# Attention scores of 27 row tiles as two-part float16 products, in a fused attention and feed-forward kernel

## The chip, the cores and the metric

The kernel runs on one core of one Trainium2 chip. The metric is the device time of one execution in microseconds (us), lower is better. Engine names are those of the profile: PE is TensorE's matmul stream, PEld its weight loads, DVE is VectorE, ACT is ScalarE, POOL is GpSimd, SP is SyncE, whose queue issues nearly all the DMAs.

## The reference

Batch 8, 8 heads, 576 rows, head size 64, model width 512. Keys and values are averaged over groups of 8 rows, so each head has 72 pooled keys. The attention is joined over the heads, normalized per row, and put through a feed-forward layer of width 2048 with a residual. All inputs are float32 in effect.

```
k_p = k.reshape(B, H, 72, 8, D).mean(axis=3);  v_p likewise
attn = softmax(q @ k_p^T / sqrt(D))
x = (attn @ v_p), heads joined to rows of 512
xn = (x - mean) / sqrt(var + 1e-6) * g
out = x + relu(xn @ w1) @ w2
```

## The kernel before

**Tiling.** The 4608 rows are 36 row tiles of 128; four tiles make a chunk of 512, so there are 9 chunks. A batch has 576 rows, which is four and a half tiles: of the 36 tiles, 32 lie in one batch, and tiles 4, 13, 22 and 31 straddle two. Each product of the feed-forward layer is done in float16 with both operands split into a high and a low part, three matmuls for one; from chunk 2 on the first layer, and from chunk 3 on the second, go through a seven-product scheme on halves (`slot`, line 792, matmuls at line 727; `slot2`, line 933, matmuls at line 950). Chunks 0 and 1 use the plain form (lines 1015 and 1050).

**The scores.** `load_q` (line 439) brings a tile of q, already transposed by the host to 128 rows (two heads of 64) by 4 pairs by 128 columns, in float32. `scores` (line 443) does one float32 matmul per pair of heads against `kblk`, which holds the pooled k of the pair as two blocks of 64 by 72 on a diagonal with zeros beside them: 128 rows by 144 columns. So a tile takes 4 matmuls, and a straddling one 8, of 64 rows of q each, in which the two batches alternate. DVE then takes the row maximum (line 458) and subtracts it (line 461); `probs` (line 468) applies the exponential on ACT (line 470), splits the result into two float16 parts (lines 481 to 497), and hands it to a DMA transpose (line 500). `values` (line 525) multiplies by the pooled v, in float16, with 16 matmuls per tile (lines 537 and 538), normalizes and forms the input of the feed-forward layer, which another DMA transpose turns (lines 614 and 637).

**Pooled k.** For batches 0 and 1 PE pools k (line 1146). For batches 2 to 7 `reduce_k` (line 1077) sums on DVE what `load_k` brought, one pair of heads at a time, and copies the two blocks into `kblk` with two ACT copies (line 1087).

**All-partition maximum.** `all_max` (line 287) rounds a column to powers of two on DVE, spreads it with one small matmul into a bank of the pool `ps_f` (line 294), and reduces it on DVE (line 303). It serves the scales of the weights and of v. The pool `ps_f` has four PSUM banks, which the feed-forward matmuls also use.

**The order.** Nothing is scheduled by the compiler. Each operation is a Python generator that yields between its steps, and the string `START` (lines 56 to 201) lists, token by token, which operation does its next step. The order of the tokens is the order of each engine's queue and of SP's DMA queue. `A.t` steps through the scores and probabilities of tile t, `B.t` through its values, `HK.b.i` and `HV.b.i` prepare half of a batch's k and v, `U` and `E` are the feed-forward products, and `D` streams parts of the second weights in through SP (line 925). `A.t` begins with the load of q for tile t + 2 (line 1070).

```
def stage_a(t):
    if FIRST_Q <= t + 2 < NRUN * TPC:
        load_q(t + 2)
        yield
    yield from scores(t)
    yield
    yield from probs(t)
```

Of the kernel before, what the change touches and what calls it, by code (L numbers as in the profile page):

```python
# [8 lines left out]
F32 = mybir.dt.float32  # L9
# [34 lines left out]
NPE = 2  # L44
HC = CH // 2
# [35 lines left out]
N.1.3 I.1.1 I.1.1 B.8 B.8 HK.3.1 A.10 N.1.2 HV.2.1 HV.2.1 T.1.0.1 I.1.1 T.1.0.1 HK.3.1 HK.3.1 T.1.0.1 HV.2.1
I.1.1 A.11 A.11 A.11 A.10 I.1.3 I.1.3 I.1.1 T.1.0.1 A.11 I.1.1 I.1.3 T.0.1.1 I.1.3 T.1.0.1 T.1.0.1 HV.2.1 I.1.3
HV.2.1 B.8 HV.2.1 B.8 I.1.3 T.0.1.1 I.1.3 A.12 A.12 I.1.1 HK.3.1 HK.3.1 I.1.1 I.1.1 I.1.3 A.11 A.12 B.8 A.11
HV.2.1 I.1.2 I.1.1 HV.2.1 N.1.1 T.1.0.1 HV.2.1 I.1.3 I.1.1 HK.4.0 HV.3.0 HV.3.0 HV.3.0 I.1.1 A.13 HK.4.0 A.13
HV.2.1 T.1.0.1 HV.2.1 A.12 HK.4.0 HK.4.0 O.0.1 A.13 O.0.1 O.0.1 O.0.1 B.8 I.1.0 HV.2.1 HV.2.1 HV.2.1 T.1.0.1
T.1.1 T.1.1 HV.3.0 HV.3.0 B.9 T.1.1 O.0.1 O.0.1 A.11 B.9 B.9 O.0.1 B.9 O.0.1 I.1.0 I.1.2 I.1.2 HV.3.0 HK.4.0
A.12 A.12 I.1.2 I.1.0 HV.3.0 I.1.2 I.1.2 B.9 I.1.0 I.1.0 B.10 HK.4.0 A.13 B.10 B.10 B.9 B.9 B.9 B.9 I.1.2
HV.3.0 B.9 B.9 I.1.0 A.12 I.1.0 I.1.0 A.13 B.10 I.1.2 O.0.1 B.11 I.1.0 B.10 B.10 I.1.0 B.10 I.1.2 B.9 I.1.0
I.1.2 B.9 HV.3.1 HV.3.1 T.1.1 I.1.0 O.1.0 B.11 I.1.2 I.1.2 U.2.1.1 B.11 B.11 A.14 F.0.0.0 A.13 A.13 O.1.0 O.1.0
U.2.0.1 HV.3.1 T.0.1.1 T.0.1.1 HV.3.1 HV.3.1 F.0.0.0 B.11 F.0.0.0 HV.3.1 F.0.0.0 B.11 F.0.0.0 B.11 B.11 B.11  # L90
HV.4.1 U.2.0.1 O.1.0 B.11 O.1.0 U.2.1.1 U.2.1.2 B.11 B.11 U.2.0.2 F.0.0.0 F.0.0.0 F.0.0.0 HV.4.1 HV.4.1 F.0.0.0
F.0.0.0 F.0.0.0 O.1.0 O.1.0 B.11 HV.4.1 F.0.0.0 U.2.1.5 U.2.0.2 U.2.0.2 B.13 O.1.0 HV.4.1 HV.4.1 HV.4.1 U.2.1.2
F.0.1.1 F.0.1.1 U.2.1.6 U.2.1.5 U.2.1.3 T.1.1 U.2.1.6 U.2.1.6 U.2.0.6 U.2.1.2 HV.4.1 F.0.1.1 F.0.1.1 O.1.1
HV.4.0 U.2.1.3 U.2.0.6 U.2.1.3 U.2.1.3 HV.4.0 HV.4.0 HV.4.0 U.2.1.7 F.1.0.1 U.2.1.7 F.1.0.1 F.1.0.1 F.1.0.1
U.2.0.5 U.2.0.6 F.1.0.1 U.2.0.5 U.2.0.7 O.1.1 U.2.1.7 U.2.0.7 U.2.1.7 U.2.0.7 F.1.0.1 HV.4.0 U.2.0.3 O.1.1
U.2.0.7 HV.4.0 U.2.0.3 U.2.0.3 U.2.0.3 HV.4.0 HV.4.0 O.1.1 F.1.0.1 F.1.0.1 F.1.0.1 F.1.0.1 O.1.1 F.1.0.1 O.1.1
U.2.2.1 U.2.0.4 U.2.0.4 F.1.0.1 U.2.2.1 HV.4.1 N.1.0 F.1.1.0 O.1.1 F.1.1.0 U.2.0.4 F.1.1.0 F.1.1.0 F.2.0.0
O.1.1 F.2.0.0 O.1.1 U.2.2.2 O.1.1 F.2.0.0 F.2.0.0 F.2.0.0 F.2.0.0 F.2.0.0 U.2.2.2 U.2.2.2 F.2.0.0 F.2.0.0 O.1.1
F.2.0.0 U.2.2.6 U.2.2.6 U.2.2.6 F.2.0.0 F.2.1.1 B.12 HV.4.1 F.2.0.0 U.2.1.4 B.13 B.13 U.2.3.1 U.2.3.1 F.2.1.1
F.2.1.1 U.2.2.7 F.3.0.1 B.13 U.2.3.2 U.2.3.2 A.14 HV.4.1 HV.4.1 O.1.1 F.2.1.1 U.2.3.2 B.12 A.14 U.2.2.5 P.2.2.0  # L100
U.2.1.4 U.2.1.4 HV.4.1 HK.4.1 U.2.2.5 U.2.2.7 A.14 U.2.2.7 U.2.2.7 P.2.2.0 B.12 U.2.3.5 F.3.0.1 F.3.0.1 A.14
A.14 U.2.3.6 F.3.0.1 U.2.3.5 HV.4.1 HV.5.0 F.3.0.1 U.2.2.4 A.14 B.13 B.12 U.2.3.6 B.12 B.12 U.2.3.3 U.2.3.3
B.12 A.15 U.2.3.6 A.15 B.13 U.2.3.7 U.2.3.7 A.15 A.15 HV.5.0 U.2.2.4 B.13 P.2.0.0 B.13 B.13 B.13 B.13 U.2.3.4
B.13 U.2.3.7 U.2.3.7 B.14 F.3.0.1 P.2.0.0 A.16 N.0.3 F.3.0.1 U.2.3.3 U.2.3.4 U.2.3.4 U.2.3.3 A.15 A.15 B.14
# [12 lines left out]
B.16 HK.6.0 U.3.2.2 B.17 B.17 E.3.0.6 B.17 U.3.2.3 E.3.0.5 A.19 U.3.2.7 B.17 U.3.2.2 B.17 B.17 A.19 HV.5.1
# [86 lines left out]


@with_exitstack
def attn_ffn_kernel(ctx: ExitStack, tc: tile.TileContext, qT, kn, vn, kT, v, g, w1, w2, out):
    nc = tc.nc

    const = ctx.enter_context(tc.tile_pool(name="const", bufs=1))  # L210
# [1053 lines left out]
```

## Time and profile before

| what | value |
|---|---|
| median of 3 runs | 817.8 us (817.46 to 817.96) |
| span of the profiled execution | 817.1 us |
| PE busy | 794.2 us, 97% of the span |
| DVE busy | 632.6 us, 77% |
| ACT busy | 459.4 us, 56% |
| POOL busy | 297.8 us, 36% |
| mean granted TensorE clock | 0.983 of full |

The span runs from the first to the last instruction of the one profiled execution. The three runs are timed without a profile and differ from that span by what lies around it, 0.7 us at the median. An engine's busy time is the union of its instructions; a matmul's length in the trace reaches to its modelled end, so the pace of matmuls is read from the distance between two starts, not from their length.

### The profile page before, as it was taken

How to read it: one execution, taken by the hardware profiler on the slowest of the kernel's cores; microseconds unless marked ns; L12 is line 12 of the kernel's file. 1: busy time of each engine (PE TensorE's matmuls, PEld its weight loads, DVE VectorE, ACT ScalarE, POOL GpSimd, SP SyncE). 2: the span in 40 equal slices, each digit the busy share in tenths (PEclk: the TensorE clock that was granted, in tenths of full speed). 3: DMA queues.
4: the chain of work that ended last, by engine and by line, in shares of the span. 5: the costliest groups of instructions: out<-in, count | busy, mean ns of one | idle time of the engine just before them, and what ended most of it. 6: DMA issues, size and time to landing. Idle time of an engine off the chain costs nothing.

```text
span 817.1 us, 16797 instructions
## 1 busy us (share of the span) xinstructions
PE 794.2 (97%) x6554; PEld 624.6 (76%) x6554; DVE 632.6 (77%) x1363; ACT 459.4 (56%) x890; POOL 297.8 (36%) x270
## 2 busy tenths in 40 slices
PE   6978999999999999999999999999999999999998
PEld 5857755544566666679889989988988899888887
DVE  1799899677866877599968898889777968976564
ACT  2699966444523362575745755756555756563442
POOL 1222456871354362234332432333322433350211
PEclk9778999999999999999999999999999999999999
DMA  9956988734642247766775586564844473543323
GB/s 324 381 194 215 265 264 264 196 106 101 121 107 101 105 112 166 177 178 166 169 171 152 145 185 156 149 166 111 172 129 93 121 165 92 120 95 97 91 65 104
DMA packets 205214, 128.49 MB, mean 157 GB/s; under 512 B 123104, under 2 KB 182480, under 8 KB 202064
## 3 DMA queue, kind: packets, MB, share of 16 engines
q1 hardware_dynamic: 204992, 127.30, 58.1%
q8 instruction: 51, 0.84, 0.4%
q14 instruction: 27, 0.22, 0.1%
q10 hardware_dynamic: 144, 0.13, 0.0%
HBM read 76.55 MB, written 19.92 MB: 118 GB/s over the span
## 4 chain that ended last, share of the span: by engine, by line
PE 89%; DVE 6%; DMA 2%; ACT 2%; issue 1%; SPq 0%; DVEq 0%; ACTq 0%
PE ps_f L727 28%; PE ps_f L950 26%; PE ps_f L1050 15%; PE ps_f L1015 9%; PE ps L448 4%; PE ps_f L1152 2%; PE ps_f L1168 1%; PE ps L537 1%; PE ps L538 1%; PE ps L535 1%; DMA w<-in_kn_dram 1%; DMA w<-d2B 1%; DMA vr<-in_v_dram 1%; DVE ring L785 1%; DVE w L310 0%
## 5 line engine op out<-in xcount | busy, mean ns | idle before, releaser
L950 PE MATMUL ps_f<-w,ring 128*128 128x256 f16 x2016 | 228.8, 273 | 1.4 <-DVE ring L772 1.2
L950 PEld LDWEIGHTS <-ring 128*128 128x128 f16 x2016 | 196.2, 98 | 25.6 <-DVE ring L772 1.9
L727 PE MATMUL ps_f<-zz,w 128*128 128x256 f16 x1344 | 159.7, 273 | 1.9 <-ACT ps_f L802 1.3
L727 PEld LDWEIGHTS <-w 128*128 128x128 f16 x1344 | 130.7, 98 | 19.4 <-issue 2.5
L1050 PE MATMUL ps_f<-w,ring 128*128 128x512 f16 x576 | 127.4, 379 | 0.0
L727 PE MATMUL ps_f<-zz,raw 128*128 128x256 f16 x1008 | 120.7, 273 | 0.0
L779 POOL TENSOR_TENSOR ring<-v,ring 128x512 f16<-128x512 f32 x48 | 56.4, 1179 | 147.9 <-ACT ring L776 113.5
L727 PEld LDWEIGHTS <-raw 128*128 128x128 f16 x1008 | 98.2, 98 | 12.8 <-issue 0.2
L1050 PEld LDWEIGHTS <-ring 128*128 128x128 f16 x576 | 56.0, 98 | 64.1
L1015 PE MATMUL ps_f<-zz,w 128*128 128x512 f16 (+1 forms) x480 | 87.3, 340 | 1.2 <-DVE allmax L303 1.2
L1015 PEld LDWEIGHTS <-w 128*128 128x128 f16 x480 | 47.1, 99 | 36.6 <-issue 1.4
L489 POOL TENSOR_TENSOR phl<-e,phl 128x512 f16<-128x512 f32 x31 | 36.1, 1163 | 87.2 <-ACT phl L481 83.8
L635 POOL TENSOR_TENSOR hl<-z,hl 128x512 f16<-128x512 f32 x28 | 33.6, 1215 | 72.1 <-ACT hl L633 70.1
L563 ACT ACTIVATE x<-ps,rs 128x64 f32<-128x64 f32 x144 | 33.3, 316 | 32.5 <-DVE x L555 24.4
L448 PE MATMUL ps<-kblk,q 128*128 128x144 f32 (+1 forms) x320 | 45.1, 306 | 4.6 <-issue 3.7
L448 PEld LDWEIGHTS ps<-kblk,q 128*128 128x128 f32 (+1 forms) x320 | 40.0, 191 | 8.3 <-issue 6.3
L577 ACT ACTIVATE z<-x,nb,y 128x512 f32<-128x512 f32 x36 | 29.3, 815 | 30.3 <-DVE nb L572 30.1
L779 POOL TENSOR_TENSOR ring<-ring 128x512 f16<-128x512 f32 x24 | 28.2, 1176 | 49.1 <-ACT ring L776 45.1
L1090 DVE TENSOR_REDUCE vp<-vr 72x64 f32<-72x512 f32 x48 | 32.4, 675 | 10.2 <-DMA vr<-in_v_dram 10.0
L776 ACT CAST ring<-v 128x512 f16<-128x512 f32 x48 | 29.6, 618 | 7.6 <-DVE v L785 3.7
L481 ACT CAST phl<-e 128x1024 f16<-128x1024 f32 x31 | 32.4, 1046 | 2.3 <-DMA pt<-phl 1.4
L517 DVE TENSOR_SCALAR a<-y,ve 128x1 f32<-128x1 f32 x108 | 29.5, 273 | 3.9
(174 smaller groups left out, 1307.1 us busy)
## 6 DMA issues: line engine op xcount, KB each, us to landing
w<-d2T SPq DMA_DIRECT2D x28, 512.0 KB
raw<-in_w_dram SPq DMA_DIRECT2D x12, 1024.0 KB
w<-d2B SPq DMA_DIRECT2D x24, 512.0 KB
q<-in_qT_dram SPq DMA_DIRECT2D x36, 256.0 KB
out_dram<-x SPq DMA_DIRECT2D x32, 256.0 KB
kr<-in_kT_dram SPq DMA_DIRECT2D x24, 288.0 KB
vr<-in_v_dram SPq DMA_DIRECT2D x48, 144.0 KB
ring<-in_w_dram SPq DMA_DIRECT2D x4, 1024.0 KB
```

What stands on the lines that cost most here:

```text
L448: nc.tensor.matmul(ps[r, p // 2, p % 2 * 2 * KV : (p % 2 + 1) * 2 * KV], lhsT=q[:, p, r], rhs=kblk[b % NKB][:, p, :], start=True, stop=True,)
L481: nc.scalar.copy(out=ph[:, :, :, 0:KA], in_=e[:, :, 0:KA].unsqueeze(1).broadcast_to([P, 2, H, KA]))
L489: nc.gpsimd.tensor_tensor(out=ph[:, 0, :, KA:P], in0=e[:, :, 0:KA], in1=ph[:, 0, :, 0:KA], op=ALU.subtract)
L563: nc.scalar.activation(out=xh[:, 4 + i, :], in_=px[:, 1, i, 0:D], func=AF.Copy, scale=rs[:, 4 + i : 5 + i])
L635: nc.gpsimd.tensor_tensor(out=hl[:, 1, r], in0=part, in1=hl[:, 0, r], op=ALU.subtract)
L727: nc.tensor.matmul(ps[:, j], lhsT=w_form(wb, int(m == 2), k)[:, fs], rhs=z_form(za, int(m == 1), k), start=(first and i == 0 and j == 0), ...
L776: nc.scalar.copy(out=hi, in_=src)
L779: eng.tensor_tensor(out=lo, in0=src, in1=hi, op=ALU.subtract)
L950: nc.tensor.matmul(parts[i], lhsT=h[:, hp, f, i * P : (i + 1) * P], rhs=w[:, f // FPB, wp, f % FPB], start=(first and f == k == 0 and (i = ...
L1015: nc.tensor.matmul(ps, lhsT=w[:, part, fs], rhs=zT[:, kz, cols], start=(n == 0), stop=(n == 3 * NKT - 1),)
L1050: nc.tensor.matmul(ps, lhsT=h[:, part, i, cols], rhs=w[:, wp, j], start=(n == 0), stop=(n == 3 * NFT // 2 - 1),)
L1090: nc.vector.tensor_reduce(out=vp[b][:, h, 0:D], in_=vraw.pop((b, h)), axis=AX.X, op=ALU.add,)
```

## The change

Tiles 0 to 8 (batches 0 and 1) keep the float32 scores. From tile 9 (`HQ`) on, q comes in by rows (`qn`, 128 rows by 512) and is split on the chip: the new operation `QS.t` (`split_q`) sums the absolute values of each row on ACT, makes a power-of-two scale per row on DVE, writes the scaled high part in float16 on ACT and the low part on DVE, side by side for each head (64 columns high, 64 low), and turns the 128 by 1024 result with a DMA transpose on SP's queue. `KS.b` (`split_k`) does the like with the pooled k of a batch, with one scale per batch through `all_max`: high and low parts go to the rows of the head's own half, and two DMAs copy them to the other half. A head's scores are then two accumulating float16 matmuls with the same 128 by 128 weights (the high part of q over its low part) and 72 columns each: first the high part of k, then its low part. There are no zero blocks. The scales come out in the exponential, whose factor is now a column made by one more DVE instruction per segment. `reduce_k` writes into a tile that holds all four pairs and no longer needs its ACT copies.

`START` is a new order throughout, from the first line on. It has the tokens of before, less the steps that fell away (27 of the `A` steps, the loads of q, and 36 of `HK`), plus 6 tokens for each of `QS.9` to `QS.35` and `KS.2` to `KS.7`. The flags that choose an engine (the last number of some tokens) are the same for every operation. `QS.t` takes three buffers of the pool tile `q` (rows of q, split q, turned q), and the pool has three.

```
+HQ = 9
...
+    def split_q(t):
+        q = q_tile()
+        nc.sync.dma_start(out=q, in_=qn[t])
+        yield
+        e, s = wk3.tile([P, 1], F32, name="qe"), scalar_tile("s1")
+        hl = q_tile()
+        nc.scalar.activation(out=hl, in_=q, func=AF.Abs, accum_out=e)
+        qe[t] = e
+        yield
+        pow2_floor(e, e)
+        pow2_inverse(s, e, 13)
+        yield
+        hl = hl.bitcast(F16).rearrange("p (h a d) -> p h a d", a=2, d=D)
+        q = q.rearrange("p (h d) -> p h d", d=D)
+        nc.scalar.activation(out=hl[:, :, 0], in_=q, func=AF.Copy, scale=s)
+        yield
+        nc.vector.scalar_tensor_tensor(
+            out=hl[:, :, 1], in0=q, scalar=s, in1=hl[:, :, 0], op0=ALU.mult, op1=ALU.subtract
+        )
+        yield
+        q_sb[t] = qt = q_tile().bitcast(F16).rearrange("p (h n) -> p h n", n=P)
+        nc.sync.dma_start_transpose(out=qt, in_=hl.rearrange("p h a d -> p (h a d)"))
...
+    def scores_f16(t):
+        q = q_sb.pop(t)
+        ps = ps_2.tile([P, 2, 512], F32, name="ps_2")
+        for r, b in segments(t):
+            k = k_parts(b)
+            for h in range(H):
+                o = ps[r, h // 4, h % 4 * KV : (h % 4 + 1) * KV]
+                for a in range(2):
+                    nc.tensor.matmul(o, lhsT=q[:, h, r], rhs=k[:, a, h], start=(a == 0), stop=(a == 1))
+        return ps
...
     def scores(t):
+        ps = scores_f32(t) if t < HQ else scores_f16(t)
         yield
...
         nc.vector.tensor_reduce(out=mx, in_=sc, axis=AX.X, op=ALU.max)
+        if t >= HQ:
+            for r, b in segments(t):
+                nc.vector.tensor_scalar(
+                    out=qe[t][r], in0=qe[t][r], scalar1=EXP_SCALE * 2.0**-26, scalar2=CK[b][r],
+                    op0=ALU.mult, op1=ALU.mult,
+                )
...
-        nc.scalar.activation(out=e, in_=e, func=AF.Exp, scale=EXP_SCALE)
+        nc.scalar.activation(out=e, in_=e, func=AF.Exp, scale=EXP_SCALE if t < HQ else qe.pop(t))
...
     def stage_a(t):
-        if FIRST_Q <= t + 2 < NRUN * TPC:
+        if FIRST_Q <= t + 2 < HQ:
...
-        kp = wk1.tile([P, DM // 2], F32, name="zs")[:, :KV]
...
-            nc.scalar.copy(out=kblk[b % NKB][r, p, c], in_=kp[r])
+        nc.vector.tensor_reduce(out=kp_all[:, p], in_=kr, axis=AX.X, op=ALU.add)
+
+    def split_k(b):
+        m, s = scalar_tile("mv"), scalar_tile("sv")
+        nc.vector.tensor_reduce(out=m, in_=kp_all, axis=AX.XY, op=ALU.max, apply_absolute_value=True)
+        e = yield from all_max(m)
+        pow2_inverse(s, e, 13)
+        CK[b] = wk3.tile([P, 1], F32, name="ck")
+        nc.vector.tensor_copy(out=CK[b], in_=e)
+        yield
+        k = k_parts(b).rearrange("q a (p j) k -> q j a p k", j=2)
+        rows = [slice(j * D, (j + 1) * D) for j in range(2)]
+        for j, r in enumerate(rows):
+            nc.scalar.activation(out=k[r, j, 0], in_=kp_all[r], func=AF.Copy, scale=s[r])
+        yield
+        for j, r in enumerate(rows):
+            nc.vector.scalar_tensor_tensor(
+                out=k[r, j, 1], in0=kp_all[r], scalar=s[r], in1=k[r, j, 0], op0=ALU.mult, op1=ALU.subtract
+            )
+        yield
+        for j, r in enumerate(rows):
+            nc.sync.dma_start(out=k[rows[1 - j], j], in_=k[r, j])
...
-        "qT": q.transpose(1, 3, 0, 2).reshape(NPAIR, P, NTT, P).transpose(2, 1, 0, 3),
+        "qT": q.transpose(1, 3, 0, 2).reshape(NPAIR, P, NTT, P).transpose(2, 1, 0, 3)[:HQ],
+        "qn": q.transpose(0, 2, 1, 3).reshape(NTT, P, DM),
```

## Rows read from the trace of the kernel before

**Rows 1.** The page, part 1: busy time, share of the span, instructions.

```profile
PE 794.2 (97%) x6554; PEld 624.6 (76%) x6554; DVE 632.6 (77%) x1363; ACT 459.4 (56%) x890; POOL 297.8 (36%) x270
```

**Rows 2.** Stretch, its length, then busy PE, PEld, DVE, ACT, POOL; clock, DMA share, GB/s.

```profile
0.00:120.00 120.00, 103.87 (x657) 79.50 (x658) 92.29 (x195) 87.94 (x150) 40.19 (x39) 0.89 0.82 271
120.00:300.00 180.00, 179.98 (x1130) 102.48 (x1129) 138.02 (x296) 82.97 (x162) 92.57 (x69) 1.00 0.51 139
300.00:700.00 400.00, 398.38 (x3727) 342.82 (x3726) 327.51 (x731) 237.65 (x482) 135.48 (x136) 1.00 0.61 149
```

**Rows 3.** The page, part 4: the chain that ended last, by engine.

```profile
PE 89%; DVE 6%; DMA 2%; ACT 2%; issue 1%; SPq 0%; DVEq 0%; ACTq 0%
```

**Rows 4.** PE in order of time, 560 to 600 us: scores and what follows them.

```profile
564.77 1.15 PE L448 MATMUL ps<-kblk,q 128*128 128x144 f32 x8
565.75 1.47 PE L727 MATMUL ps_f<-zz,w 128*128 128x256 f16 x12
567.06 5.72 PE L950 MATMUL ps_f<-w,ring 128*128 128x256 f16 x48
...
597.31 1.20 PE L448 MATMUL ps<-kblk,q 128*64 128x144 f32 x16
598.44 1.48 PE L727 MATMUL ps_f<-zz,w 128*128 128x256 f16 x12
```

**Rows 5.** PE in order of time, 444 to 445 us: `all_max`, then one tile's values.

```profile
444.34 0.20 PE L294 MATMUL ps_f<-ident,rowmax 72*128 72x72 bf16 x1
444.38 0.19 PE L537 MATMUL ps<-va,pt 128*128 128x65 f16 x1
...
444.86 0.19 PE L538 MATMUL ps<-vb,pt 88*128 88x65 f16 x1
444.89 0.27 PE L950 MATMUL ps_f<-w,ring 128*128 128x256 f16 x1
```

**Rows 6.** PE in order of time, 466 to 468 us: values of straddling tile.

```profile
466.14 0.22 PE L537 MATMUL ps<-va,pt 128*64 128x65 f16 x1
...
467.19 0.50 PE L727 MATMUL ps_f<-zz,w 128*128 128x256 f16 x3
```

**Rows 7.** Groups by line and shape, DVE: busy us, mean ns, idle before.

```profile
L520 DVE TENSOR_SCALAR y<-a,y 128x1 f32<-128x1 f32 x108 | 23.1, 214 | 3.8
L772 DVE SCALAR_TENSOR_TENSOR ring<-v,ring 128x512 f16<-128x512 f32 x24 | 16.9, 704 | 0.7 <-ACT ring L770 0.7
L310 DVE SCALAR_TENSOR_TENSOR vb<-vp,sv,vh 72x512 f16<-72x512 f32 x7 | 5.9, 842 | 1.2 <-ACT vh L308 1.2
L272 DVE TENSOR_SCALAR rowmax<-rowmax 72x1 int32<-72x1 int32 x7 | 1.0, 150 | 0.2
```

**Rows 8.** Groups by line and shape, ACT: busy us, mean ns, idle before.

```profile
L633 ACT CAST hl<-z 128x512 f16<-128x512 f32 x28 | 17.1, 619 | 10.7 <-DVE z L626 5.4 <-DMA out_dram<-x 3.7 <-DVE z L628 1.6
L1087 ACT COPY kblk<-zs 64x72 f32<-64x72 f32 x48 | 11.9, 247 | 10.5 <-DVE zs L1081 10.3
L357 ACT ACTIVATION_READ_ACCUMULATOR raw<-w 128x1 f32 x12 | 2.3, 190 | 0.0
```

**Rows 9.** Busy time in two stretches of 20 us, columns as in rows 2.

```profile
440.00:460.00 20.00, 20.00 (x196) 18.16 (x194) 18.41 (x44) 12.60 (x26) 6.23 (x6) 1.00 0.67 180
540.00:560.00 20.00, 20.00 (x196) 18.06 (x195) 18.13 (x44) 10.03 (x18) 6.41 (x6) 1.00 0.62 155
```

**Rows 10.** Transposes of line 614 on SP: duration ns min/median/max, first and last start.

```profile
L614 SPq DMA_TRANSPOSE zz<-hl x14: 1232/1256/1815, 182.9 to 720.3; - x14
```

**Rows 11.** SP's queue, its longest wait: what ended it, us, times, longest.

```profile
SPq L925 <- PE ps_f L950: 93.2, 23, 9.7
```

**Rows 12.** The page, part 3: the DMA queue, packets, MB, share of 16 engines.

```profile
q1 hardware_dynamic: 204992, 127.30, 58.1%
```

**Rows 13.** PE's longest waits: what it waited for, us, times, longest.

```profile
PE ps_f L1152 <- DMA w<-in_kn_dram: 6.9, 1, 6.9
...
PE ps_f L950 <- DVE ring L772: 1.2, 2, 0.9
```

More of the change, by code (lines that the diff above doesn't have):

```diff
@@ L206, in attn_ffn_kernel @@
 @with_exitstack
-def attn_ffn_kernel(ctx: ExitStack, tc: tile.TileContext, qT, kn, vn, kT, v, g, w1, w2, out):
+def attn_ffn_kernel(ctx: ExitStack, tc: tile.TileContext, qT, qn, kn, vn, kT, v, g, w1, w2, out):
     nc = tc.nc
@@ L241, in attn_ffn_kernel @@
     ]
-    pool_w = const.tile([P, 2 * D + P // POOL], F32, name="pool_w")
+    kp_all = const.tile([P, NPAIR * KV], F32, name="kp_all")
+    pool_w = kp_all[:, : 2 * D + P // POOL]
+    kp_all = kp_all.rearrange("p (a k) -> p a k", k=KV)
     ones = pool_w[:, D : D + P // POOL]
@@ L424, in split_v @@
             nc.sync.dma_start(out=VB[b][KV + i * KR : KV + (i + 1) * KR], in_=vh[KA:])
[L427 removed]
+    q_sb, E, PT, X, Z, zTs, qe, CK = {}, {}, {}, {}, {}, {}, {}, {}
     def segments(t):
@@ L441, in load_q, with q_tile, k_parts, scores_f32 @@
         nc.sync.dma_start(out=q_sb[t], in_=qT[t])
-    def scores(t):
+    def q_tile():
+        return wk3.tile([P, NPAIR, P], F32, name="q").rearrange("p a n -> p (a n)")
+    def split_q(t):
[20 more added lines that the diff above has]
+        nc.sync.dma_start_transpose(out=qt, in_=hl.rearrange("p h a d -> p (h a d)"))
+    def k_parts(b):
+        k = kblk[b % NKB].rearrange("p a k -> p (a k)").bitcast(F16)
+        return k.rearrange("p (a h k) -> p a h k", a=2, k=KV)
+    def scores_f16(t):
[8 more added lines that the diff above has]
+        return ps
+    def scores_f32(t):
         q = q_sb.pop(t)
@@ L454, in scores @@
                 )
+        return ps
+    def scores(t):
+        ps = scores_f32(t) if t < HQ else scores_f16(t)
         yield
@@ L1079, in reduce_k @@
         kr = kraw.pop((b, p))
-        kp = wk1.tile([P, DM // 2], F32, name="zs")[:, :KV]
-        nc.vector.tensor_reduce(
-            out=kp, in_=kr, axis=AX.X, op=ALU.add
-        )
-        yield
-        for j in range(2):
-            r, c = slice(j * D, (j + 1) * D), slice(j * KV, (j + 1) * KV)
-            nc.scalar.copy(out=kblk[b % NKB][r, p, c], in_=kp[r])
+        nc.vector.tensor_reduce(out=kp_all[:, p], in_=kr, axis=AX.X, op=ALU.add)
[6 more added lines that the diff above has]
+        nc.vector.tensor_copy(out=CK[b], in_=e)
+        yield
+        k = k_parts(b).rearrange("q a (p j) k -> q j a p k", j=2)
[10 more added lines that the diff above has]
+            nc.sync.dma_start(out=k[rows[1 - j], j], in_=k[r, j])
     def reduce_v(b, h):
@@ L1100, in prep_k @@
             yield
-            yield from reduce_k(b, p)
+            reduce_k(b, p)
             yield
@@ L1216, in attn_ffn_kernel @@
         "LK": rows_k, "LV": rows_v, "G": load_g, "K": pe_k, "V": pe_v, "R": load_raw,
-        "Q": load_q, "A": stage_a, "B": values, "C": convert, "M1": max_w1, "M2": max_w2, "S": split_w, "E": slot2, "D": w2_stream, "J": w2_resident,
+        "Q": load_q, "QS": split_q, "KS": split_k, "A": stage_a, "B": values, "C": convert, "M1": max_w1, "M2": max_w2, "S": split_w, "E": slot2, "D": w2_stream, "J": w2_resident,
         "F": w2_forms, "N": keep_w2, "OUT": put_out,
```

287 lines of the change are left out of this document (142 added, 145 removed).

## The prediction, made before the changed kernel ran

> **What bounds the kernel now.** I read the page's busy times first: PE is busy 97% of the span, no other engine above 77% [rows 1]. A busy PE can still be a slow one, so I then read the stages. From 120 to 700 us PE has no gaps to speak of: 398.4 of 400 us in the long middle, at the full granted clock [rows 2]. Only the first 120 us are loose, with 16 us of idle PE and a mean clock of 0.89, while DVE and ACT are at 77% and 73% and DMA at 82%: four resources near their limits together. The chain of waits says the same, 89% PE [rows 3], and PE's waits are the first load, 6.9 us, and little else: behind DVE's evictions of the middle it loses 1.2 us in all [rows 13]. So in the middle a microsecond taken from PE is a microsecond gained, as long as DVE, busy 327.5 of those 400 us [rows 2], keeps up.
>
> The profiled execution spans 817.1 us; the median of the runs is 817.8, so I add 0.7 at the end.
>
> **PE.** In the middle a whole tile's float32 scores start at 564.77 and the next work at 565.75: 0.98 us for 4 matmuls, each in two records. A straddling tile takes 598.44 less 597.31, 1.13 us [rows 4]. The new form has 16 matmuls per whole tile, float16, 128 by 128 weights, 72 columns. The nearest thing in the trace is one tile's values: 16 float16 matmuls of 65 columns, each with its own weight load, from 444.38 to 444.89, that is 0.51 us or 32 ns each [rows 5]. For 7 more columns at the 2.4 GHz of this stretch I add 3 ns: 35 ns, 0.57 us per tile. Bounds: 0.51 us (columns don't count) and 16 x 109 ns = 1.75 us (every one at the pace of the 256-column matmuls behind that tile, 12 of them from 565.75 to 567.06 [rows 4]). I take 0.57, because the row with the same type, weights and nearly the same width is much the nearest. Gain 0.41 us for each whole tile. A straddling tile becomes 32 matmuls on 64 columns of weights; 32 such in the values take 467.19 less 466.14, 1.05 us [rows 6], so about 1.15 with the wider rows: nothing gained, since the old ones alternated between two batches and were cheap already.
>
> Of tiles 9 to 35, three straddle (13, 22, 31) and 24 don't: 24 x 0.41 = 9.8 us off PE. The six new `all_max` matmuls take 444.38 less 444.34, 0.04 us each [rows 5], 0.2 us in all. Net 9.6 us.
>
> The Trainium skill, TensorE: Matmul & The Clock Gate, section "Back-to-back issue gap", speaks against that: a stream of weight load and matmul pairs is said to sustain about 81 ns per matmul at 128 columns, far above the time of the columns. By it a tile would take some 1.3 us (an estimate from that page), and nothing would be gained. This case's values run at 32 ns with a weight load for each, so the trace doesn't agree.
>
> **DVE.** Added per tile: three small instructions for the power of two (0.15 each by the masking one), the low part of 128 by 512 (0.70), the factor of the exponential (0.21) [rows 7]: 1.36 us, and 0.21 more on straddling tiles. 27 x 1.36 + 0.6 = 37 us. Per batch `KS` adds eight DVE instructions, at least 0.15 and at most 0.84 each [rows 7]; four are single columns, and the other four are bounded by both ends, so 1.2 to 4.0 us; I take 2.3, six batches 14 us. `reduce_k` sums as before. In all 51 us, DVE goes from 633 to 684 us. About 20 of the 27 tiles and four batches fall in the middle, 35 us: 362 us of DVE against 400 less 8 us of PE, 92.5%. In the two densest stretches of before DVE ran 18.41 and 18.13 of 20 us (92% and 91%) with PE at 20.00 [rows 9]. So the load fits, with no slack. I charge 2 us for PE waiting on late evictions; bounds 0 and the DVE rival below.
>
> **ACT.** Added per tile: sum of absolute values and scaled copy (0.62 each by the float16 cast of that size) and the accumulator's read (0.19): 27 x 1.43 = 39 us. Removed: 48 copies, 11.9 us [rows 8]; 12 scaled copies of k come back, bounded by 0.25 and 0.62, say 5. ACT ends near 491 us of 810, 61%. I cost this at nothing because DVE and PE are both denser; without that cover it would be 32 us.
>
> **DMA and SP.** The loads of q are as many and as large as before; they are `QS` tokens now. New are 27 transposes of 1024 columns, 1.26 us each on SP by line 614's [rows 10], 34 us of issue, and 12 small copies of k. SP's queue has slack: its second-weight loads alone stand 93 us waiting for PE to free their place [rows 11]. 1024 packets of 256 B per transpose make 27,648, 13% more than the queue's 204,992 at 58.1% [rows 12], so DMA goes to at most 66%. I cost both at nothing.
>
> **New waits.** `QS` waits for its q on ACT, for ACT on DVE, for DVE on SP, and PE's scores wait for the turned q and, once per batch, for the copies of k. Behind the waiting scores on PE stands the whole feed-forward stream; behind the waiting transpose on SP stand the w2 loads, v loads and outputs. The three q buffers hold about one tile in the making. The chain of five steps takes some 10 us if each queue serves it within 2 us, and a tile comes every 18 us or so (400 us for 22 tiles), so there is room. In the new order the first `QS` token of a tile stands at a median of 36 us of PE work ahead of its scores (token list, priced by rows 4 to 6), and 0 to 28 us lie after its transpose. The few at zero are where I would look for gaps; the old order puts some `B` tokens as close behind their transposes, and no wait on them shows among PE's longest [rows 13].
>
> **The new order early on.** The tokens before the first feed-forward work are the same in sum (41 to 45 us of PE work, 42 to 43 of DVE, 47 of ACT). I take no change; with 16 us of idle PE there and half clock in parts, it may be 5 us either way.
>
> **Sum.** 817.1 - 9.6 + 2 + 0.7 = 810.2, say 810.
>
> **The rivals.**
>
> *DVE becomes the bound (slower).* Place: 300 to 700 us. It decides if DVE can't be kept above 362/400 = 90.5% busy over the whole stretch, since below that the stretch grows past its 400 us. At 88% the stretch is 412 us and the time 817.8 + 12 - 2 (the tiles before it) = 828; at the 82% of now it would be 442 us and 858. For it: dependent hops between ACT and DVE, which no order removes. Against: 92% with PE full in [rows 9]. Chance 0.11.
>
> *The gain is handed back (no change).* Turned q comes late or SP's queue blocks the w2 loads: a wait of 0.35 us in each of the 27 tiles is 9.5 us. Time 813 to 819, centre 817. For it: a chain of five queues with three buffers. Against: the distances above. Chance 0.14.
>
> *The change doesn't shorten the matmuls.* If each small matmul goes at the pace of its weight load rather than of its columns, by the upper bound a whole tile costs 0.77 us more and a straddling one 32 x 0.109 - 1.13 = 2.4 more: 817.8 + 18.5 + 7 = 843; halfway, 824. Against: rows 5. Chance 0.03. The skill's 81 ns would give about 830.
>
> *The new order also closes early gaps.* A third of the 16 idle us goes: 803 to 805. Chance 0.10.
>
> **How the numbers follow.** Forecast 0.62, at 810 (806 to 813 by itself). Some 0.2% (1.6 us) is what a measurement can tell from no change: faster means below 816.2, slower above 819.4. Faster: 0.62 + 0.10 + 0.08 of the handed-back case = 0.80. No change: the other 0.06. Slower: 0.11 + 0.03 = 0.14. The range goes from 804 to 818.5: it leaves out the slower cases and the best of the early-gap case, about 0.2.
>
> **What would show it right or wrong.** Right: 16 score matmuls of 128x72 f16 some 35 ns apart, a tile's scores 0.57 us; PE busy down by 9 to 10 us; DVE 680 to 690 us and ACT about 490; PE still above 99% in the middle. Wrong: small matmuls 60 ns apart or more; PE waiting several us in all for DVE's evictions (lines 748, 772, 779, 785) or for a transposed q; a first 120 us with more or less PE work done than now.

## The result, and the profile after

Time after: 807.8 us median (804.3 to 809.2, four runs), against 817.9 (817.5 to 818.0) beside it. The ratio is 0.9867 with a 95% interval of 0.9844 to 0.9890, so the change saves 9 to 13 us. A second set on another chip gave 806.0 against 818.7, ratio 0.9835 (0.9817 to 0.9853). Forecast were 810, with 804 to 818.5 as the range. The profiled execution took 807.3 us; its span of 805.6 stands against 817.1. Of the experiments below, three hold one execution that is a quarter to several times longer than its neighbours (the old form of the scores, the maximum replaced, the scaled copy three times), which their medians and ratios leave out.

The page's busy times, its DMA queue and the engines' shares of the chain that ended last, after the change:

```profile
PE 781.4 (97%) x6800; PEld 610.4 (76%) x6800; DVE 675.2 (84%) x1549; ACT 489.1 (61%) x935; POOL 306.1 (38%) x270
...
q1 hardware_dynamic: 239840, 135.26, 64.9%
...
PE 78%; DVE 11%; DMA 5%; ACT 4%; issue 1%; POOL 0%; SPq 0%; DVEq 0%; ACTq 0%
```

Against [rows 1, 3, 12]: PE is busy 12.8 us less, its idle time went from 22.9 to 24.2 us (span less busy), and the difference is the 11.5 us of the span. The chain tells what the time alone doesn't: PE's share fell from 89% to 78%, and DVE, DMA and ACT hold 20% of it, where they had 10. The kernel still ends on PE, but other engines are on its path far more often.

The same by stage, columns as in [rows 2]:

```profile
0.00:120.00 120.00, 106.11 (x659) 77.43 (x660) 91.44 (x201) 88.10 (x149) 31.67 (x35) 0.90 0.79 274
120.00:300.00 180.00, 175.60 (x1249) 100.50 (x1247) 157.54 (x362) 92.43 (x179) 102.31 (x73) 1.00 0.65 162
300.00:700.00 400.00, 397.81 (x3956) 341.67 (x3955) 362.32 (x864) 263.65 (x527) 146.36 (x140) 1.00 0.70 162
```

In the long middle DVE went from 327.5 to 362.3 us (90.6%) and PE still has only 2.2 us of gaps. New gaps stand between 120 and 300 us, 4.4 us where there were none; the first 120 us have 2.2 fewer than before.

What the change was made for, PE in order of time: a whole tile's scores and what follows them, two times, then a straddling tile's (compare [rows 4]).

```profile
530.23 0.68 PE L482 MATMUL ps<-kblk,q 128*128 128x72 f16 x16
530.74 1.48 PE L779 MATMUL ps_f<-zz,w 128*128 128x256 f16 x12
...
550.91 0.68 PE L482 MATMUL ps<-kblk,q 128*128 128x72 f16 x16
551.43 1.48 PE L779 MATMUL ps_f<-zz,w 128*128 128x256 f16 x12
...
395.01 1.12 PE L482 MATMUL ps<-kblk,q 128*64 128x72 f16 x32
396.07 0.21 PE L295 MATMUL ps_f<-ident,rowmax 72*128 72x72 bf16 x1
```

From start to start a whole tile takes 0.51 to 0.52 us, 32 ns for each of its 16 matmuls, where the float32 form took 0.98. A straddling tile takes 1.06 instead of 1.13.

The largest groups of the new steps by line and shape: busy us, mean ns, idle before. First PE's scores (float16 at line 482, what is left of float32 at line 490), then the low part of q on DVE and its scaled copy on ACT.

```profile
L482 PE MATMUL ps<-kblk,q 128*128 128x72 f16 x384 | 16.4, 198 | 0.0
L482 PE MATMUL ps<-kblk,q 128*64 128x72 f16 x96 | 3.4, 200 | 0.0
L490 PE MATMUL ps<-kblk,q 128*128 128x144 f32 x64 | 11.2, 328 | 0.8 <-ACT x L615 0.8
L490 PE MATMUL ps<-kblk,q 128*64 128x144 f32 x16 | 2.2, 454 | 0.0
...
L463 DVE SCALAR_TENSOR_TENSOR q<-q,s 128x512 f16<-128x512 f32 x27 | 22.3, 827 | 1.8 <-ACT q L461 1.7
...
L461 ACT ACTIVATE q<-q,s 128x512 f16<-128x512 f32 x27 | 19.5, 722 | 9.6 <-DVE s L279 9.5
```

PE's scores before, as groups:

```profile
L448 PE MATMUL ps<-kblk,q 128*128 128x144 f32 x256 | 39.3, 299 | 0.9 <-ACT kblk L1162 0.9
L448 PE MATMUL ps<-kblk,q 128*64 128x144 f32 x64 | 5.8, 332 | 3.7 <-issue 3.7
```

The scores sum to 33.2 us of PE instead of 45.1 (39.3 + 5.8). PE waited for nothing in front of the new ones: their idle time is 0.0.

PE's longest waits after (what it waited for, us, times, longest; before in [rows 13]):

```profile
PE ps_f L1218 <- DMA w<-in_kn_dram: 6.7, 1, 6.7
PE ps_f L640 <- ACT z L629: 4.3, 2, 2.8
PE ps_f L1102 <- DVE w L311: 2.3, 2, 1.5
PE ps_f L295 <- DVE ring L1081: 1.6, 1, 1.6
```

None of them is for a turned q or a copy of k. The first is the load at the start, as before. The second, PE's transposes of the first tiles waiting for ACT at about 57 and 61 us, has no like before. The fourth is the new `all_max` of a batch's k at 181.8 us (128 by 128, like the five other new ones; those of v are 72 by 72), held until DVE was through with an eviction of line 1081. So one of the new steps does make PE wait, for 1.6 us. The third is new too. Three more views show its cause: the split of the second weights in the profile of before (ns, min/median/max), then DVE in order of time, then POOL, around 140 us after the change.

```profile
L310 DVE SCALAR_TENSOR_TENSOR w<-w,ws x8: 1271/1276/1305, 107.2 to 145.1; 128x1024 f16<-128x1024 f32 x8
```

```profile
139.37 3.27 DVE L311 SCALAR_TENSOR_TENSOR w<-w,ws 128x1024 f16<-128x1024 f32 x1
142.55 0.67 DVE L1156 TENSOR_REDUCE vp<-vr 72x64 f32<-72x512 f32 x1
143.85 1.85 DVE L311 SCALAR_TENSOR_TENSOR w<-w,ws 128x1024 f16<-128x1024 f32 x1 [0.62 <-ACT w L309]
```

```profile
138.29 1.16 POOL L650 TENSOR_TENSOR hl<-z,hl 128x512 f16<-128x512 f32 x1 [7.00 <-ACT hl L648]
139.41 2.14 POOL L726 TENSOR_TENSOR w<-w 128x1024 f32<-128x1024 f16 x1
141.63 2.99 POOL L729 TENSOR_TENSOR w<-w 128x1024 f32<-128x1024 f32 x1
```

The split of the second weights on DVE, 1.27 to 1.31 us each in the profile of before, took 3.27 and 1.85 here. POOL's sum of line 726 ends at 139.41 + 2.14 = 141.55, and 1.09 us behind that the first of them is done; line 729 ends at 144.62, and the second is done 1.08 behind that. So the new order put a DVE instruction with two inputs in SBUF beside POOL instructions that read SBUF, and by these ends DVE stood until POOL was through. The Trainium skill, SBUF — State Buffer, section "Who interferes with whom", says that a DVE instruction with two SBUF inputs contends with a GpSimd instruction that reads SBUF, and calls it an exclusive lock; the 3.27 us agree with it.

### The profile page after: what moved, and what is told of

Its sections match the earlier page's. It is cut to its first block, busy times and chain, and to the rows that moved or that the text cites. A ratio compares the mean times of both kernels' runs of the same rounds, so it can differ in the third digit from the quotient of the medians.

```text
span 805.6 us, 17573 instructions
## 1 busy us (share of the span) xinstructions
PE 781.4 (97%) x6800; PEld 610.4 (76%) x6800; DVE 675.2 (84%) x1549; ACT 489.1 (61%) x935; POOL 306.1 (38%) x270
## 3 DMA queue, kind: packets, MB, share of 16 engines
q1 hardware_dynamic: 239840, 135.26, 64.9%
## 4 chain that ended last, share of the span: by engine, by line
PE 78%; DVE 11%; DMA 5%; ACT 4%; issue 1%; POOL 0%; SPq 0%; DVEq 0%; ACTq 0%
PE ps_f L779 30%; PE ps_f L1002 24%; PE ps_f L1102 10%; PE ps_f L1067 6%; DMA vr<-in_v_dram 2%; DVE w L311 2%; PE ps L482 1%; PE ps_f L1218 1%; PE ps L589 1%; PE ps_f L1234 1%; PE ps L590 1%; PE ps L587 1%; DMA kr<-in_kT_dram 1%; DMA w<-in_kn_dram 1%; DVE vp L1156 1%
## 5 line engine op out<-in xcount | busy, mean ns | idle before, releaser
L1067 PE MATMUL ps_f<-zz,w 128*128 128x512 f16 (+1 forms) x480 | 85.2, 336 | 0.7 <-DVE w L311 0.7
L504 DVE TENSOR_REDUCE mx<-ps 128x8 f32<-128x576 f32 x36 | 27.0, 750 | 11.9 <-PE ps L490 8.5
L343 POOL TENSOR_SCALAR raw<-raw 128x1024 int32<-128x1024 uint16 x12 | 14.5, 1208 | 48.9 <-DMA raw<-in_w_dram 39.7
```

Source lines behind the costliest of these rows:

```text
L1067: nc.tensor.matmul(ps, lhsT=w[:, part, fs], rhs=zT[:, kz, cols], start=(n == 0), stop=(n == 3 * NKT - 1),)
```

## The experiments

Three theories. **PE**: the gain is the shorter scores, in a kernel that PE bounds. **DVE**: DVE is now a bound too, and hands part of it back or is near doing so. **Order**: the order found anew brings time of its own. Times of different chips are compared through the kernel before beside them, 818 to 819 us each time.

**The old form of the scores in the new kernel.** All of the new preparation runs in the new order, but the scores use the float32 matmuls of before on the bits that lie there, so that scores, and output, are others. (The exponent of both scales, of q and of k, is made smaller, to keep the numbers finite.)

```diff
-        pow2_inverse(s, e, 13)
+        pow2_inverse(s, e, 3)
...
-        for r, b in segments(t):
-            k = k_parts(b)
-            for h in range(H):
...
+        q = q.rearrange("p h n -> p (h n)").bitcast(F32).rearrange("p (a n) -> p a n", n=P)
+        for p in range(NPAIR):
+            for r, b in segments(t):
+                nc.tensor.matmul(
+                    ps[r, p // 2, p % 2 * 2 * KV : (p % 2 + 1) * 2 * KV],
+                    lhsT=q[:, p, r],
+                    rhs=kblk[b % NKB][:, p, :],
...
```

> The changed kernel, with one thing undone: from tile 9 on the scores are again 4 float32 matmuls of 144 columns per whole tile (8 on a straddling one), reading the bits of the split q and k as float32, so they are no scores; the power-of-two scales are 2^10 smaller to keep them finite. All splits, transposes, DVE and ACT work and the whole new order stay. Theory PE (the gain is PE's shorter scores): 24 whole tiles x (0.98 - 0.51) + 3 x 0.1 = 11.5 us more than the changed kernel, about 819. Rival ORDER (a good part of the gain is the new order): at most half of that, 813 or less.

Measured: 817.7 us median of nine, ratio 0.9988 (0.9974 to 1.0002). Its scores in PE's order of time, and its long middle:

```profile
535.14 1.15 PE L480 MATMUL ps<-kblk,q 128*128 128x144 f32 x8
536.13 1.47 PE L783 MATMUL ps_f<-zz,w 128*128 128x256 f16 x12
...
300.00:700.00 400.00, 398.96 (x3717) 342.57 (x3716) 355.83 (x853) 258.80 (x515) 142.78 (x138) 1.00 0.70 159
```

With scores of 0.99 us the whole gain is gone. So the net gain is PE's. This run also prices all that was added: 45 us of DVE (677.6 against 632.6 busy), 30 of ACT, 27 transposes and a new order together come to no change (0.9974 to 1.0002). It gives their sum only: what the new order brings by itself may be offset by what the new steps cost. In its profile PE is idle for 27.8 us instead of the 22.9 of before, and the mean clock of the first 120 us is 0.96 instead of 0.89. So Order falls as the source of the net gain, not as a term within it.

**Every score matmul twice.** The second pair starts its sum anew, so the result is the same.

```diff
-                for a in range(2):
+                for a in (0, 1, 0, 1):
```

> The changed kernel with every float16 score matmul done twice over (start, accumulate, start, accumulate), same result. Theory PE: 24 x 0.51 + 3 x 1.05 = 15.4 us more, about 823. Rival DVE (DVE at 90% of the middle sets the time, PE fills in): PE would have slack for it, under 8 us more.

Measured: 824.1 us, ratio 1.0071 (1.0049 to 1.0092), some 17 us above the changed kernel.

```profile
539.39 1.20 PE L482 MATMUL ps<-kblk,q 128*128 128x72 f16 x32
540.43 1.48 PE L779 MATMUL ps_f<-zz,w 128*128 128x256 f16 x12
...
300.00:700.00 400.00, 399.38 (x4199) 343.48 (x4198) 355.12 (x844) 257.82 (x513) 139.25 (x135) 1.00 0.70 158
```

32 matmuls take 1.04 us, 0.52 more than 16. Over 24 whole and 3 straddling tiles that is 24 x 0.52 + 3 x 1.06 = 15.7 us, and nearly all that the time rose by (on the page PE's busy time rose by 14.8, from 781.4 to 796.2). PE's time counts about in full, in both directions. With PE longer, DVE has slack again: 355 of 400 us, and PE's gaps in the middle shrink to 0.6.

**The low part of q twice on DVE.**

```diff
-        nc.vector.scalar_tensor_tensor(
-            out=hl[:, :, 1], in0=q, scalar=s, in1=hl[:, :, 0], op0=ALU.mult, op1=ALU.subtract
-        )
+        for _ in range(2):
+            nc.vector.scalar_tensor_tensor(
+                out=hl[:, :, 1], in0=q, scalar=s, in1=hl[:, :, 0], op0=ALU.mult, op1=ALU.subtract
+            )
```

> The changed kernel with the low part of q written twice on DVE: 27 x 0.65 = 17.5 us of DVE more, 13 of it in the middle, which brings DVE from 362 to about 375 of 400 us there. Theory PE: DVE still fits, 0 to 3 us more, at most 811. Rival DVE: the added work comes out in full, about 17 us more, 825.

Measured: 825.7 us, ratio 1.0082 (1.0050 to 1.0114): 17.9 above 807.8. The doubled group and two stretches of it:

```profile
L464 DVE SCALAR_TENSOR_TENSOR q<-q,s 128x512 f16<-128x512 f32 x54 | 48.6, 900 | 2.7 <-ACT q L461 1.7
...
120.00:300.00 180.00, 170.89 (x1184) 95.03 (x1183) 159.34 (x360) 93.05 (x180) 102.17 (x72) 1.00 0.66 165
300.00:700.00 400.00, 389.16 (x3834) 328.89 (x3832) 371.97 (x858) 254.84 (x508) 143.63 (x135) 1.00 0.70 159
```

DVE gets to 372 of 400 us, 93.0%; PE now stands 10.8 us in the middle and 9.1 before it, in many waits of 0.2 to 2.5 us: 10.5 of these 20 us for DVE, 3.4 for ACT, 5.7 for DMAs, of which 0.9 for turned q, which the second write makes later. The group rose by 26.3 us (48.6 against 22.3) and DVE's busy time by 26.1, more than the 17.5 expected, since the 54 writes took 900 ns on average. So 26 us more of DVE cost 18. The theory that PE alone binds, whatever DVE does, falls.

**The low part of q left out.** ACT writes the high part into both halves.

```diff
-        nc.scalar.activation(out=hl[:, :, 0], in_=q, func=AF.Copy, scale=s)
+        nc.scalar.activation(out=hl, in_=q.unsqueeze(2).broadcast_to([P, H, 2, D]), func=AF.Copy, scale=s)
...
-        nc.vector.scalar_tensor_tensor(
-            out=hl[:, :, 1], in0=q, scalar=s, in1=hl[:, :, 0], op0=ALU.mult, op1=ALU.subtract
-        )
```

The changed kernel ran once more beside it, as it stands:

> The changed kernel once more, as the yardstick for the three beside it. Both theories: 808 us, about 10 under the kernel before.

> The low part of q is left out of the computation (both halves hold the high part): 17.5 us less DVE, about 12 us more ACT, PE's work the same. If the changed kernel is bound by PE alone, with DVE only just keeping up, it gains no more than the gaps that DVE causes: 0 to 4 us (804 to 808). If DVE is a second bound of the middle, on which every us counts as in the run with the low part twice, it gains 8 to 10 us (798 to 800).

Measured: 806.0 us and 801.3; ratios 0.9835 (0.9817 to 0.9853) and 0.9781 (0.9758 to 0.9805). DVE's busy time fell by 18.4 us, so 18 us less of DVE are worth about 5, against 18 for 26 us more. Where the 5 lie: the page's busy times and the first two stretches, first of the changed kernel, then without the low part.

```profile
PE 781.7 (97%) x6800; PEld 610.3 (76%) x6800; DVE 675.6 (84%) x1549; ACT 488.3 (61%) x935; POOL 305.3 (38%) x270
...
0.00:120.00 120.00, 105.31 (x655) 76.98 (x656) 90.66 (x200) 87.48 (x147) 30.90 (x35) 0.90 0.80 271
120.00:300.00 180.00, 175.92 (x1250) 100.73 (x1249) 157.14 (x361) 92.67 (x181) 103.11 (x73) 1.00 0.67 164
```

```profile
PE 775.5 (97%) x6800; PEld 606.0 (76%) x6800; DVE 657.2 (82%) x1522; ACT 499.3 (62%) x935; POOL 300.3 (38%) x270
...
0.00:120.00 120.00, 102.07 (x679) 74.07 (x680) 93.15 (x203) 89.89 (x150) 32.32 (x35) 0.96 0.81 277
120.00:300.00 180.00, 178.76 (x1276) 102.66 (x1273) 154.35 (x362) 97.92 (x184) 101.90 (x73) 1.00 0.66 160
```

Both have 6,800 matmuls and both leave PE idle for 23.9 us (805.6 - 781.7 and 799.4 - 775.5), but not at the same place. Without the low part PE is idle 17.9 us in the first 120 instead of 14.7, at a better clock (0.96 against 0.90), and has done 24 more matmuls there. Behind 120 us it is idle 6.0 us instead of 9.3 (the rest of the span less the rest of the busy time). So of the 6.2 us between the two spans, 3.3 are waits that went behind 120 us, most of them between 120 and 300, and 2.9 are the matmuls done sooner. The waits that went there are the two of the section above, for the split of line 311 (2.3 us) and for the eviction ahead of `all_max` (1.6).

The clock alone doesn't explain the difference of the times either. The changed kernel's four executions beside this run took 807.3, 806.7, 803.7 and 805.4 us at mean clocks of 0.984, 0.985, 0.989 and 0.994; without the low part it was 802.9 at 0.985, and 801.1, 798.1 and 801.4 at 0.994. At like clocks 4 to 7 us remain. Whether the smaller load on DVE, the shorter way of q or another meeting of instructions brought them isn't taken apart by this run: the edit changes all three.

**Two other ways to relieve DVE, with the sum of absolute values and the layer norm.** The first gives the same result: the maximum in the power of two becomes a bias, and the factor of the exponential goes to ACT.

```diff
...
-        nc.scalar.activation(out=hl, in_=q, func=AF.Abs, accum_out=e)
+        nc.scalar.activation(out=hl, in_=q, func=AF.Abs, bias=tiny, accum_out=e)
...
-        pow2_floor(e, e)
+        nc.vector.tensor_single_scalar(
+            out=e.bitcast(I32), in_=e.bitcast(I32), scalar=EXP_BITS, op=ALU.bitwise_and
+        )
...
-                nc.vector.tensor_scalar(
-                    out=qe[t][r], in0=qe[t][r], scalar1=EXP_SCALE * 2.0**-26, scalar2=CK[b][r],
-                    op0=ALU.mult, op1=ALU.mult,
-                )
+                nc.scalar.activation(out=qe[t][r], in_=qe[t][r], func=AF.Copy, scale=CK[b][r])
...
```

> The same result with less DVE: the maximum in the power of two is replaced by a bias of 1e-30 in the sum of absolute values, and the factor of the exponential goes from DVE to ACT. DVE 11 us less, ACT 6 us more, PE the same. If PE alone binds: 0 to 3 us less (805 to 808). If DVE binds too: 5 to 7 us less (801 to 803).

Measured: 803.4, 804.2 and 808.7 us, ratio 0.9837 (0.9804 to 0.9869), as the changed kernel beside it (0.9835). DVE fell by 6.6 us, where the instructions taken away sum to 10 by their groups: the busy share counts overlapping records once, and some other groups grew. The second, alone and together with the first:

```diff
-        for _ in range(3):
+        for _ in range(2):
             nc.vector.tensor_scalar(
                 out=a, in0=y, scalar1=ve, scalar2=y, op0=ALU.mult, op1=ALU.mult
             )
```

(Two steps instead of three also turn the sign of the root.)

> The reciprocal root of the layer norm takes two Newton steps and not three: 72 small DVE instructions less, 36 x (273 + 214) ns = 17.5 us of DVE, and nothing added anywhere. It is the same relief as with the low part of q left out, without that run's 12 us of extra ACT. If DVE's density costs PE a few us in the middle: 800 to 802. If that run's gain came from its early clock (0.96 against 0.90 in the first 120 us) and not from DVE: 804 to 808.

> Both reliefs of DVE together, 24 us. If PE is nearly full once DVE has slack, the second adds little: 799 to 802. If DVE still decides: 795 to 798.

Measured: 802.8 us, ratio 0.9835 (0.9797 to 0.9872), and 803.6, ratio 0.9832 (0.9802 to 0.9862), on another chip than the changed kernel's 0.9835, and no different from it. DVE's busy time is 663.1 and 654.5 us, 12 and 21 less. In the middle DVE comes down to 355 and 350 of 400 us, and PE's gaps there are 1.4 and 2.2 us as in the two profiles of the changed kernel (1.4 and 2.2). So at 362 us DVE doesn't hold PE up in the middle yet. Behind 120 us PE is idle 7.8 and 8.0 us instead of 9.3 and 10.3, which is all that the relief can be seen to bring. None of these three versions is clearly faster than the changed kernel.

**The low part of q on POOL.**

```diff
-        nc.vector.scalar_tensor_tensor(
-            out=hl[:, :, 1], in0=q, scalar=s, in1=hl[:, :, 0], op0=ALU.mult, op1=ALU.subtract
-        )
+        nc.gpsimd.tensor_scalar(out=q, in0=q, scalar1=s, scalar2=None, op0=ALU.mult)
+        nc.gpsimd.tensor_tensor(out=hl[:, :, 1], in0=q, in1=hl[:, :, 0], op=ALU.subtract)
```

> The changed kernel with the low part of q taken from DVE to POOL in two steps (scale in place, then subtract): 17.5 us of DVE less, 27 x 2 x 1.18 = 64 us of POOL more (306 to 370 of 806), the low part 1.7 us later. Theory PE: only PE's gaps of 120 to 300 us (4.4 us) are there to win, so 0 to 4 us less, 804 to 808. Rival DVE: 10 us less or more, under 798.

Measured: 826.6 us, ratio 1.0088 (1.0060 to 1.0115), which no theory had. Its long middle, and POOL's two new groups:

```profile
300.00:700.00 400.00, 388.05 (x3826) 329.19 (x3824) 344.62 (x820) 254.38 (x505) 189.01 (x170) 1.00 0.70 157
...
L463 POOL TENSOR_SCALAR q<-q,s 128x512 f32<-128x512 f32 x27 | 46.4, 1717 | 69.1 <-ACT q L461 37.8 <-DVE ring L836 13.6 <-DVE v L933 7.5
...
L464 POOL TENSOR_TENSOR q<-q 128x512 f16<-128x512 f32 x27 | 32.8, 1216 | 2.2
```

DVE is down to 86% and POOL is busy under half of the stretch, yet PE stands 12 us. On POOL the step takes 1.72 + 1.22 = 2.9 us per tile where DVE took 0.83. So busy share isn't all that binds: a step that comes 2 us later in each tile, on a queue with other work, costs as much as a full DVE. A part can be read from the run without the low part, which takes the same instructions off DVE: DVE is busy 657.2 us there and 666.0 here, so 8.8 us are other instructions of DVE taking longer beside a busier POOL. What the later q and the evictions queued behind it on POOL cost was not taken apart.

**ACT: the scaled copy of q three times.**

```diff
-        nc.scalar.activation(out=hl[:, :, 0], in_=q, func=AF.Copy, scale=s)
+        for _ in range(3):
+            nc.scalar.activation(out=hl[:, :, 0], in_=q, func=AF.Copy, scale=s)
```

> The scaled copy of q is made three times on ACT, 54 instructions and about 38 us of ACT more, to 65% of the span; everything else as it was. If ACT's new work costs nothing because PE and DVE are the denser engines, as the prediction had it: 805 to 810. If the chain ACT, DVE, ACT, DVE, SP of a tile's q, or ACT's evictions behind it, have no slack: 815 to 825.

Measured: 817.0 us, ratio 0.9986 (0.9967 to 1.0005): the gain is gone, some 10 us for 39 us of ACT (54 x 0.72). ACT's work was not covered for more than it is. The copies also bring each tile's q 1.4 us later, and no profile of the run at its usual time exists, so whether ACT's share or the later q costs the 10 us isn't seen.

**SP: each transpose of q twice.**

```diff
-        nc.sync.dma_start_transpose(out=qt, in_=hl.rearrange("p h a d -> p (h a d)"))
+        for _ in range(2):
+            nc.sync.dma_start_transpose(out=qt.rearrange('p h n -> p h n'), in_=hl.rearrange("p h a d -> p (h a d)"))
```

> Each transpose of q is issued twice: 27 more of 1.2 to 1.3 us on SP's queue and 27,648 packets more. If SP and the DMA queue have slack, as the prediction had it: 805 to 810. If turned q or SP's queue holds PE (the rival in which the gain is handed back): 815 to 830, with PE waiting for a transposed q, for w2 loads or for turned z.

Measured: 851.9 us, ratio 1.0425 (1.0397 to 1.0452), 44 us above the changed kernel. Some of its longest waits, of SP's queue and of PE:

```profile
SPq L469 <- DMA q<-q: 61.3, 28, 4.2
...
PE ps L483 <- DMA q<-q: 8.0, 5, 3.4
...
PE ps_f L1003 <- DMA w<-d2B: 5.7, 3, 3.0
PE ps_f L780 <- DMA zz<-hl: 5.4, 2, 4.3
```

The second transpose writes where the first does, and SP waits for the first to land: 61.3 / 28 = 2.2 us per tile, beside the 1.25 of issue. So this run prices SP's queue being held, and q coming, 3.4 us later per tile, not the issue alone. PE then waits for turned q, for w2 loads and for turned z: the very waits of the rival in which the gain is handed back.

**The old token order, with the new steps put in by a rule.** The tokens, and with them the work, are the same; each `QS` and `KS` is put as far ahead of its scores as its load allows.

```diff
...
-I.0.1.0 I.0.2 I.0.1.0 HV.2.0 I.0.1.1 X.0 HV.2.0 I.0.1.0 I.0.2 I.0.1.1 B.4 T.0.0.1 I.0.2 I.0.2 A.8 C.2.5.1.1 A.7 QS.9
...
+B.4 X.1 S.2.0 HK.2.1 S.2.0 KS.2 HV.2.0 HV.2.0 B.5 KS.2 QS.9 T.0.0.1 T.0.0.1 A.7 T.0.0.1 T.0.0.1 B.4 B.4 I.0.3 N.0.0
...
```

> The token order of the kernel before, with the new steps put in by one rule: each scale of q and each of k as far ahead of its scores as its load allows, the same work on every engine. If the order found anew is what lets DVE, SP and PE keep step, this costs: 812 to 830. If the shorter scores carry the gain whatever the order, it stays at 806 to 811.

Measured: 919.1 us, ratio 1.1225 (1.1208 to 1.1242). PE's two longest waits:

```profile
PE ps_f L275 <- DVE rowmax L253: 18.4, 5, 8.1
PE ps L462 <- DMA q<-q: 16.6, 5, 8.3
```

PE stands for the new steps themselves: for `all_max` of k, whose token makes PE's queue wait on DVE (16.4 of the 18.4 us; the other 2.0 are there before the change too), and for turned q. This placing is one bad order, not the best for the old tokens, so the 113 us are no price of the old order. They show what the steps cost where their distances are not looked after.

## Why the prediction was right, point by point

**What bounds the kernel: right.** PE's scores carry the net gain; put back, the time is 817.7. The granted clock doesn't: at about the mean clock of before (0.983) the changed kernel's executions took 809.2 us (0.982) and 807.3 (0.985).

**PE: right, its term a little small.** Predicted were 9.6 us. The matmuls of 72 columns run 32 ns apart, as those of 65 do, so the 3 ns added for seven more columns were not due, and the lower bound of 0.51 us was the value. By the starts it is 24 x (0.98 - 0.51) = 11.3 and 3 x 0.07 = 0.2 for the straddling tiles, for which "nothing gained" was put; the groups of scores give 45.1 - 33.2 = 11.9. PE as a whole has 12.8; the last microsecond isn't assigned. So PE fell by more than the 9 to 10 us named as a sign. From 810.2 to the measured 807.8, 3.2 us are PE and 0.7 its waits; against them stand 1.5, since the median lies 2.2 us above the span of the profiled execution here, where 0.7 was added. The rule of the Trainium skill, TensorE: Matmul & The Clock Gate, section "Back-to-back issue gap" (81 ns for each pair of weight load and matmul at 128 columns), would have the new scores slower than the old: the trace has 32.

**The 2 us for PE waiting: right in size by luck, wrong in place.** PE's idle time rose by 1.3 us, but in the middle, where the charge was put, by 0.6. It rose by 4.4 between 120 and 300, where the prediction had no term, and fell by 2.2 before and 1.7 at 700 to 780. Of the 4.4, 2.3 are DVE standing beside POOL, which the prediction did not look for, and 1.6 the new `all_max`, whose wait on DVE it had not priced.

**DVE: right.** Forecast were 362 of 400 us in the middle; 362.3 were measured. On the page it rose by 42.6 us and not by 51, to 675 instead of the 680 to 690 named as a sign. The instructions by their own groups sum to 55 more; the busy share counts overlapping records once (the groups add up to 728 us, the page says 675). The low part took 827 ns on average instead of the 704 of [rows 7]: most took 744, some up to 1,642.

**The rival in which DVE becomes the bound: its mechanism was right, and it was nearer than a chance of 0.11 says.** It was to decide where DVE can't be kept above 90.5%. DVE stands at 90.6% with PE at 99.5%, which less DVE doesn't better, and in the run with the low part twice, at 93%, PE falls to 97.3%. So the ceiling lies between the two, the margin is at most 2.4 points of 400 us, 10 us, and 26 us more of DVE cost 18.

**ACT, SP and DMA at nothing: right for what was added, wrong as slack.** ACT ended at 489 us (491 predicted), the DMA queue at 64.9% (at most 66). The run with the old form of the scores shows that all of it together, in the new order, cost nothing. But the cover that ACT was given ends soon, or the way of q has no slack: the tripled copy costs 10 us of its 39. And "SP's queue has slack" was read from its wait for PE, 93 us in [rows 11]. That was no slack for q: holding the queue and q 3.4 us longer per tile costs 44 us.

**The gain handed back: didn't come by that way.** No wait for turned q is among PE's longest, and the idle time ahead of the new scores is 0.0. The transposes doubled, and the old order with the steps put in, show it as it would have been.

**Early gaps closed: in part.** A third of 16 us was named. The first 120 us have 13.9 us of idle PE instead of 16.1 at nearly the same clock; 4.4 us behind them took it back.

## What to carry to other kernels

Where PE is full, price a change of its matmuls by the distance of starts in the nearest rows of the same type; here two-part float16 with four times the matmuls took half the time of float32 padded with zeros. Then ask of every other engine not whether it has slack on the page, but how far its densest stretch is from the highest share seen with PE full: this kernel's DVE had room for what was added and for little more. And ask how late a new step makes the chain that it stands in. A wait that a queue spends is not slack for a new step that stands in the middle of a chain; test it by delaying that step.

## What the runs showed of the hardware

- Matmuls of 65 and of 72 columns, each with a weight load of its own, run at the same 32 ns; the seven columns more cost nothing.
- A DVE instruction of 1.28 us took 3.27 where it had two inputs in SBUF and POOL was reading. Before, none of the eight of its group took more than 1.31, with the same instructions in another order.
- The granted clock early in the program differs for almost the same work; over the whole span it was 0.982 to 0.994 in eight executions of the changed kernel. Two rows each, of the changed kernel and of the version with the maximum replaced, 40 to 48 us:

```profile
40.00:44.00 4.00, 3.86 (x13) 2.19 (x11) 3.71 (x11) 3.61 (x8) 0.79 (x1) 0.50 0.38 147
44.00:48.00 4.00, 4.00 (x15) 2.77 (x15) 3.54 (x17) 4.00 (x10) 0.33 (x1) 0.50 0.64 229
```

```profile
40.00:44.00 4.00, 4.00 (x19) 2.36 (x18) 3.68 (x12) 3.59 (x10) 1.03 (x1) 0.72 0.35 137
44.00:48.00 4.00, 4.00 (x25) 2.94 (x24) 3.61 (x15) 3.97 (x9) 0.11 (x1) 1.00 0.72 272
```

In the one PE holds 1.2 GHz (0.50) over these 8 us, in the other it is back at 2.4 GHz (1.00) from 44 us on, though PE had been equally busy from 28 to 40 us in both, 10.97 of 12 us. Little of that is won: by 60 us PE has been busy 49.8 us in the one and 44.8 in the other, but has done 257 and 261 matmuls, because the faster one then stands, most of it for ACT's normalized rows of the first tiles. By 120 us it is 25 matmuls ahead, about 2 us of PE by what is left of its busy time. Nor do the times follow the mean clock: the eight executions of the changed kernel took 809.2, 807.3, 807.3 and 806.7 us at 0.982 to 0.985, 804.3 and 803.7 at 0.987 and 0.989, and 808.4 and 805.4 at 0.992 and 0.994. A gain of a few us should be read from PE's busy and idle time stage by stage: the sums over the span can hide a wait that went in one place and came in another.
